# A searched order of steps and a rearranged prologue in a block-sparse attention and low-rank mixer kernel

## The chip, the cores and the metric

The kernel runs on one core of a Trainium2 chip. The core has TensorE (PE), VectorE (DVE), ScalarE (ACT), GpSimd (POOL) and SyncE (SP), and DMA queues that some of these issue to. The metric is the device time of one launch in microseconds. The median of three runs of the kernel before is 270.56 us (269.94 to 271.41).

## The reference

```python
scores = (1 / sqrt(64)) * q @ k.T            # 4 batches, 8 heads, 768 tokens, 64 channels
mask: blocks of 32 tokens; own block and both neighbours, first and last row and column of
      blocks, and three sampled blocks for each row of blocks
attn = softmax(where(mask, scores, -1e9)) @ v
x = attn as (batch, token, 512)
u = x + ((x.T @ U) @ V).T                    # U: 768 x 32, V: 32 x 768, over the tokens
out = u + relu(u @ w_ch1) @ w_ch2            # 512 -> 2048 -> 512
```

## The kernel before

**Tiling.** Two heads make a pair; there are 16 pairs, four for each batch. A head's 768 keys are six groups of 128 (the program's `g`), and scores are held with keys on the partitions and all 768 queries along the row. PSUM has eight banks of 512 fp32 columns; each step names the bank that it writes.

**The order of the work** is written out by hand, or by a search, in the string `PLAN`: one word for each step, from left to right, with the bank behind it where the step needs one. A capital without dots, or one of the words with dots, is TensorE's work; most lower-case letters are the VectorE or ScalarE operations that empty a bank. The program goes through the words and issues each step's instructions to its engine, so the list fixes the order on each engine; between engines only the dependencies count. A step that comes earlier in the string than one of another engine need not run earlier. The words that matter here:

- `S` (line 980) scores of one group, two banks; `B` (L999) scores of two groups, three banks; `e` the exponential of the oldest of them on ScalarE (L989, L1007). These serve pairs 0 to 3, batch 0. There the mask is added by the same matmul: below the 64 channels of `kres` stand rows with the mask's bias for each block (copied by `mask_row`, L287, out of a bank that `mask_half`, L279, fills), and below those of `qres` a one-hot row for each block.
- `A` six matmuls of a group's values (L414), `v` the division by the row sums (L544, L551).
- `R` the transposes of a later pair's queries or keys (L953), `t` their copies; `Z` those of the very first pair's second head (L352), `z` their copies (L359); `K`, `k` a part of the multiplicative mask for later batches.
- From pair 4 on: `Q` scores of one step of both heads, banks 0 to 5, on half the array's rows each (L1030), `e` the exponential (L1039), `p` the mask's multiplication on VectorE (L1045), `V` all six value products of a head.
- `M` and `D`, `E`, `F`, `X`, `Y` the mixer's products; `x`, `d` what adds and casts them in pairs 4 to 15 (L630, L634), `T` a transposing DMA of the result (SP, L623).
- `P`, `C`, `U` the up projection (L685), `a` and `b` its relu on ScalarE (L697) or VectorE (L699); with dots the last digit of `a` names the engine.
- `S`, `H`, `D` with dots: the down projection in seven products instead of eight, with sums of its inputs on VectorE (L721, L855) and the outputs' additions (L879). `q` sums of weights on VectorE, `g`, `c`, `o`, `r`, `s`, `h`, `e` with dots the last batch, where both projections are done in seven products; `t` with dots its input sums. `Z` with dots a store, `L` loads of a later pair.

**The prologue** (lines 243 to 346) stands before the list. `keep_warm` (L272) runs eight matmuls of constants. `first_cast` (L213) makes fp16 of the first head's queries and keys, `first_turn` (L227) transposes half of them with three matmuls on the identity, `first_row` (L293) copies 64 rows of the result out of the bank. Mask rows and key rows are read out of a bank partly by VectorE, partly by ScalarE. The second head of the pair is cast on GpSimd. `second_set` (L192) copies the one-hot and the mask rows to the second set of tiles by DMA from SP.

Of the kernel before, what the change touches and what calls it, by code (L numbers as in the profile page):

```python
# [12 lines left out]
FP32 = mybir.dt.float32  # L13
# [10 lines left out]
def kernel(  # L24
# [192 lines left out]
    def first_turn(n, c):  # L217

        if n == 1:
            pt = bank(5 + c, [P, HS], FP32)  # L220
        elif c == 0:
            pt = pw[:, 1, 0:HS]
        else:
            pt = psc2()[:, 0, 0:HS]
        first_out[n, c] = pt
        for j in range(3):
            nc.tensor.matmul(  # L227
                pt[0:D, j * P : (j + 1) * P],
                sts[0, ("qld", "kld")[n]][:, 3 * c + j, 0],
                id16,  # L230
                start=(j == 0), stop=(j == 2), skip_group_check=True,
            )

    with tc.manual_schedule(
# [27 lines left out]
        for vt in vts:  # L262
            nc.gpsimd.memset(vt[:, :, :, D : D + 1], 1.0)
# [12 lines left out]
        pks = [bank(2, [P, HS], FP32), bank(7, [P, HS], FP32)]  # L276
# [23 lines left out]
        keep_warm(8)  # L300
# [28 lines left out]
        mask_row(0, 1, nc.vector.tensor_copy)  # L329
        mask_row(1, 1, nc.vector.tensor_copy)  # L330
# [9 lines left out]
        load_mix_u()  # L340
        second_set()
# [117 lines left out]
    a.0.1.0.1 p a.0.1.14.1 Q v q.4.0 e V6 D.0.0.0 S.0.0.3 H.0.0.6.0 e v U.0.1.13.2 q.7.0 H.0.0.6.1
    U.0.1.12.6 a.0.1.13.1 D.0.0.2 y p Q a.0.1.12.1 q.5.1 H.0.0.7.0 e H.0.0.7.1 q.5.0 H.0.0.5.0.6 D.0.0.3  # L460
    H.0.0.5.1 e S.0.0.4.4 U.0.1.6.1 p H.0.0.4.0 a.0.1.6.1 H.0.0.4.1 D.0.0.4 Q D.0.0.5 p H.0.0.3.0 e L.7
    H.0.0.3.1 p H.0.0.2.0.7 H.0.0.2.1 e p U.0.1.8.2 U.0.1.15.0 D.0.0.1 D.0.0.6 a.0.1.8.1 V7 p a.0.1.15.1
    S.0.1.1.1 Q S.0.2.1.0 V6 e v S.0.1.2.4 H.0.1.1.0.7 y v H.0.1.1.1 y H.0.1.2.0.0 S.0.2.2.3 y H.0.1.2.1
    e D.0.1.0 M6 D.0.1.1 H.0.2.1.0.1 m H.0.2.1.1 S.0.2.3 F.1.0.2.4 D.0.2.0 F.1.1.3.6 F.1.2.5.0 x.6.0
    H.0.2.6.0 x.6.1 d.6.0 H.0.2.6.1 x.7.0 d.6.1 F.1.3.6.4 D.0.2.2 H.0.1.6.0 T.6 x.5.1 H.0.1.6.1 S.0.1.3
    H.0.2.7.0 H.0.2.7.1 x.4.0 H.0.2.5.0.6 x.5.0 H.0.2.2.0.0 D.0.2.3 d.5.0 H.0.2.2.1 x.4.1 d.5.1
    H.0.2.4.0 D.0.1.2 d.4.0 T.5 x.7.1 H.0.2.4.1 d.7.0 H.0.1.7.0 D.0.2.1 d.4.1 D.0.2.5 H.0.1.7.1 d.7.1
    S.0.2.4.2 T.4 Q D.0.1.3 H.0.2.5.1 e H.0.1.4.0 T.7 D.0.2.4 H.0.1.4.1 H.0.2.3.0 e D.0.1.5 H.0.2.3.1
    Z.0.0.1 p H.0.1.5.0.7 Z.0.2.1 H.0.1.5.1 D.0.2.6 Q Z.0.2.0 D.0.1.4 Z.0.0.0 S.0.1.4.0 U.1.0.0.6 e
    H.0.1.3.0 a.1.0.0.0 H.0.1.3.1 e U.1.0.11.6 D.0.1.6 p U.1.0.10.0 Z.0.1.0 Z.0.1.1 a.1.0.11.1 U.1.0.9.7  # L470
    p L.8 a.1.0.10.1 U.1.0.6.6 a.1.0.9.1 p Q a.1.0.6.1 p U.1.0.12.6 e V7 e U.1.0.2.2 v U.1.0.5.0 p
    a.1.0.12.1 U.1.0.1.7 a.1.0.5.1 a.1.0.2.1 U.1.0.3.6 a.1.0.1.0 p Q a.1.0.3.1 V6 p e U.1.0.4.7 v e
    U.1.1.5.2 a.1.0.4.0 U.1.0.15.6 p a.1.1.5.1 U.1.1.9.7 a.1.0.15.1 p Q a.1.1.9.1 U.1.1.3.7 e L.9
    U.1.0.7.6 a.1.1.3.0 e U.1.0.14.7 a.1.0.7.0 p U.1.1.4.0 U.1.1.10.6 a.1.0.14.1 a.1.1.4.0 U.1.1.1.7 p
    a.1.1.10.1 Q a.1.1.1.1 V7 e V6 v e U.1.1.7.7 v Q a.1.1.7.1 p U.1.0.8.7 e H.1.0.1.0.6 a.1.0.8.0
    H.1.0.1.1 p e U.1.1.13.7 p U.1.0.13.0 U.1.1.14.2 p a.1.0.13.1 a.1.1.13.1 U.1.1.8.3 S.1.0.1.3
    a.1.1.14.1 U.1.1.6.7 a.1.1.8.1 S.1.0.3 Q a.1.1.6.1 S.1.0.2.0 H.1.0.2.0.7 e D.1.0.0 L.10 H.1.0.2.1
    S.1.0.4.4 H.1.0.6.0 D.1.0.1 H.1.0.6.1 e U.1.1.15.1 U.1.1.11.0 a.1.1.15.0 U.1.1.0.7 p a.1.1.11.1 Q
    D.1.0.2 a.1.1.0.1 p y V7 e H.1.0.7.0 v e H.1.0.7.1 U.1.1.2.0 p U.1.1.12.7 D.1.0.3 a.1.1.2.1 p Q
    a.1.1.12.1 S.1.1.1.0 H.1.0.4.0 e H.1.0.4.1 S.1.1.2.1 V7 D.1.0.5 e S.1.1.3 H.1.1.1.0.6 p H.1.1.1.1 Q  # L480
    D.1.1.0 v H.1.1.6.0 e L.11 p H.1.1.6.1 H.1.0.5.0.7 D.1.1.2 H.1.0.5.1 e p H.1.1.7.0 H.1.1.7.1 D.1.0.4
    V0 y p y y H.1.1.5.0.3 S.1.1.4.3 y V4 y D.1.1.3 v H.1.1.5.1 v y H.1.1.4.0 H.1.1.4.1 S.1.2.1.1 y
    H.1.0.3.0 D.1.1.4 M4 S.1.2.2.0 H.1.0.3.1 m D.1.1.5 F.2.0.5.4 F.2.1.0.1 D.1.0.6 Z.1.1.1 H.1.2.1.0.6
    x.8.0 H.1.2.1.1 x.10.0 d.8.0 H.1.1.3.0 x.10.1 d.10.0 F.2.2.7.5 D.1.2.0 F.2.3.4.2 d.10.1 H.1.2.2.0.1
    x.8.1 T.10 H.1.2.2.1 x.11.0 H.1.1.3.1 x.9.0 d.11.0 H.1.2.6.0 x.11.1 d.8.1 H.1.2.6.1 d.9.0 D.1.1.6
    T.8 H.1.1.2.0.7 D.1.2.1 d.11.1 x.9.1 H.1.1.2.1 S.1.2.3 d.9.1 Q T.11 D.1.2.2 D.1.1.1 e H.1.2.7.0
    H.1.2.7.1 T.9 H.1.2.5.0.7 D.1.2.3 e H.1.2.5.1 S.1.2.4.2 H.1.2.4.0 Z.1.1.0 H.1.2.4.1 Z.1.0.1 Q
    D.1.2.5 D.1.2.4 U.2.0.4.6 p e H.1.2.3.0 a.2.0.4.0 H.1.2.3.1 e U.2.0.12.6 D.1.2.6 U.2.0.5.7 Z.1.2.0
    Z.1.0.0 a.2.0.12.1 Q Z.1.2.1 a.2.0.5.0 p U.2.0.2.7 e L.12 U.2.1.8.6 a.2.0.2.0 U.2.1.1.7 a.2.1.8.1 e
    U.2.0.11.2 a.2.1.1.0 U.2.0.15.6 p a.2.0.11.1 U.2.0.0.7 p Q a.2.0.0.1 p a.2.0.15.1 U.2.0.9.7 e V6  # L490
    a.2.0.9.0 p e U.2.0.8.0 v U.2.0.10.7 a.2.0.8.1 U.2.1.4.6 a.2.0.10.0 p Q a.2.1.4.1 V7 p e U.2.1.0.6 v
    e U.2.0.13.1 a.2.1.0.0 U.2.0.1.7 p a.2.0.13.1 U.2.1.2.6 a.2.0.1.1 p Q a.2.1.2.0 U.2.1.9.7 e L.13
    U.2.0.7.6 a.2.1.9.0 e U.2.0.6.7 a.2.0.7.0 p U.2.0.14.6 a.2.0.6.1 q.0.1 Q a.2.0.14.1 p V7 e q.0.0 V6
    v e q.1.1 U.2.0.3.7 v Q a.2.0.3.1 p H.2.0.1.0.7 e p U.2.1.5.6 H.2.0.1.1 S.2.0.1.4 e U.2.1.10.0
    a.2.1.5.0 U.2.1.14.1 S.2.0.2.1 a.2.1.10.0 U.2.1.3.6 a.2.1.14.1 D.2.0.0 Q S.2.0.3 a.2.1.3.1 p
    H.2.0.6.0 e H.2.0.2.0.6 p H.2.0.6.1 H.2.0.2.1 e D.2.0.2 U.2.1.13.0 D.2.0.1 S.2.0.4.3 H.2.0.7.0
    a.2.1.13.1 H.2.0.7.1 p y Q p V6 e D.2.0.3 H.2.0.4.0 v e H.2.0.4.1 V6 D.2.0.5 p Q v U.2.1.11.7 e
    H.2.0.5.0.6 a.2.1.11.0 H.2.0.5.1 q.1.0 e U.2.1.12.7 p U.2.1.15.0 p a.2.1.12.1 U.2.1.7.1 a.2.1.15.1
# [685 lines left out]
```

## Time and profile before

| | |
|---|---|
| median of three runs | 270.56 us |
| the profiled execution | 270.01 us |
| its span, first to last instruction | 268.2 us |
| mean granted TensorE clock | 0.999 |
| instructions | 7303 |
| first two-head score step | 42.76 us |
| first matmul of the last batch's up projection | 228.3 us |
| last matmul | 264.7 us |

A busy share is the time in which an engine had at least one instruction in work. TensorE's matmuls overlap: the profile gives each of them a duration of which a good part runs beside the next one. How close they follow is read from their starts. "Idle before", with an arrow, names what ended an engine's idle time. The lines are those of the program before.

### The profile page before, as it was taken

The page shows a single profiled execution, that of the slowest core. Times are in us where ns is not written, and L with a number is a line of the kernel's source. Part 1 is how long each engine was busy: PE and PEld are TensorE (multiplying, and loading weights), DVE is VectorE, ACT ScalarE, POOL GpSimd, SP SyncE. Part 2 cuts the span into 40 slices and gives each one's busy share as a digit, 9 for nine tenths or more (in the row PEclk, how much of TensorE's full clock was granted, in tenths as well). Part 3 has the DMA queues.
Part 4 walks back from the last instruction along what each step waited for, and adds up shares of the span by engine and source line. Part 5 has one row for each costly group of instructions (what it writes and reads, how often), then busy time and mean ns, then how long its engine had stood idle before and what let it go on. Part 6 is the DMA issues. An engine that isn't in the chain of part 4 may idle for free.

```text
span 268.2 us, 7303 instructions
## 1 busy us (share of the span) xinstructions
PE 262.4 (98%) x3006; PEld 182.4 (68%) x3006; DVE 232.5 (87%) x477; ACT 202.7 (76%) x265; POOL 72.7 (27%) x98
## 2 busy tenths in 40 slices
PE   8899999999999999999999999999999999999995
PEld 3677775555577778565666887555667788666884
DVE  5789988988999998868588997688998999999993
ACT  4999998897989667788898857788997944789200
POOL 4669006944462570070606160000000000000000
PEclk9999999999999999999999999999999999999999
DMA  6799997999999999897938997610200116400024
GB/s 192 245 324 263 207 235 123 113 135 144 189 146 133 117 103 111 284 98 89 90 39 67 106 109 139 223 34 13 51 0 2 42 42 117 159 2 0 2 98 137
DMA packets 88720, 31.66 MB, mean 118 GB/s; under 512 B 77104, under 2 KB 85840, under 8 KB 88688
## 3 DMA queue, kind: packets, MB, share of 16 engines
q0 software_dynamic: 49728, 10.10, 48.4%
q1 hardware_dynamic: 38492, 20.86, 33.6%
q8 instruction: 23, 0.38, 0.6%
q10 hardware_dynamic: 468, 0.26, 0.4%
q14 instruction: 9, 0.07, 0.1%
HBM read 27.67 MB, written 6.29 MB: 127 GB/s over the span
## 4 chain that ended last, share of the span: by engine, by line
PE 73%; DMA 12%; DVE 7%; ACT 2%; POOL 2%; issue 1%; SPq 0%; DVEq 0%; POOLq 0%; ACTq 0%
PE ps L760 32%; PE ps L685 17%; DMA w2t<-in_moe_w_ch_dram 9%; PE ps L414 9%; PE ps L1030 7%; DMA vld<-in_v_dram 2%; PE ps L999 2%; ACT est L1007 2%; PE ps L980 1%; DVE est L1045 1%; PE ps L272 1%; DMA qpl<-stqld 1%; PE ps L665 1%; DVE xf L551 1%; DVE res L969 1%
## 5 line engine op out<-in xcount | busy, mean ns | idle before, releaser
L1039 ACT ACTIVATE est<-ps 128x1536 f16<-128x1536 f32 x72 | 100.6, 1450 | 18.8 <-PE ps L1030 18.7
L685 PE MATMUL ps<-uT,w1t 128*128 128x384 f16 x384 | 70.2, 326 | 0.0
L1045 DVE TENSOR_TENSOR est<-est,mask 128x1440 f16<-128x1440 f16 x72 | 63.4, 903 | 0.6 <-ACT est L1039 0.2
L685 PEld LDWEIGHTS <-w1t 128*128 128x128 f16 x384 | 35.6, 97 | 26.6 <-issue 6.8
L414 PEld LDWEIGHTS <-est 128*128 128x128 f16 x1152 | 40.4, 97 | 7.0 <-issue 3.3
L414 PE MATMUL ps<-vt,est 128*128 128x65 f16 x1152 | 43.3, 193 | 0.2 <-DVE xf L551 0.2
L760 PEld LDWEIGHTS <-hid 128*128 128x128 f16 x358 | 34.0, 98 | 6.6 <-issue 1.6
L697 ACT ACTIVATE hid<-ps 128x384 f16<-128x384 f32 x63 | 29.7, 496 | 4.8 <-PE ps L685 4.3
L1030 PE MATMUL ps<-qpl,kpl 64*128 64x512 f16 (+1 forms) x288 | 31.7, 325 | 0.0
L139 POOL DMA_DIRECT2D stqld<-in_q_dram x20 | 16.3, 820 | 55.9 <-DMA qpl<-stqld 54.4
L760 PE MATMUL ps<-w2t,hid 128*128 128x256 f16 x238 | 31.1, 273 | 0.0
L879 DVE TENSOR_TENSOR xf<-xf,ps 128x256 f32<-128x256 f32 x63 | 25.4, 416 | 4.1 <-PE ps L760 3.7
L699 DVE TENSOR_SCALAR hid<-ps 128x384 f16<-128x384 f32 x33 | 18.3, 555 | 8.7 <-PE ps L685 8.0
L760 PEld LDWEIGHTS <-sums 128*128 128x128 f16 x216 | 20.1, 98 | 4.4 <-issue 1.0
L989 ACT ACTIVATE est<-ps 128x768 f16<-128x768 f32 x30 | 22.5, 812 | 0.1
L1030 PEld LDWEIGHTS <-kpl 64*128 64x128 f16 x288 | 12.3, 94 | 14.3 <-issue 9.1
L760 PE MATMUL ps<-res,sums 128*128 128x256 f16 x144 | 19.4, 273 | 0.0
L634 ACT CAST xh<-xf 128x384 f16<-128x384 f32 x24 | 11.0, 510 | 10.0 <-DVE xf L630 10.0
L551 DVE TENSOR_TENSOR xf<-ps,rcp 128x384 f32<-128x384 f32 x32 | 17.7, 554 | 0.8
L139 POOL DMA_DIRECT2D stkld<-in_k_dram x20 | 16.3, 819 | 1.9 <-issue 0.8
L139 POOL DMA_DIRECT2D vt<-in_v_dram x20 | 16.3, 820 | 0.0
L760 PE MATMUL ps<-res,hid 128*128 128x256 f16 x120 | 15.9, 273 | 0.0
(121 smaller groups left out, 339.3 us busy)
## 6 DMA issues: line engine op xcount, KB each, us to landing
out_dram<-xf SPq DMA_DIRECT2D x18, 256.0 KB, 2.4
vld<-in_v_dram SPq DMA_DIRECT2D x6, 384.0 KB, 6.3
w1t<-in_moe_w_ch_dram POOLq DMA_DIRECT2D x4, 512.0 KB, 8.3
w2t<-in_moe_w_ch_dram POOLq DMA_DIRECT2D x4, 512.0 KB, 12.1
qld<-in_q_dram SPq DMA_DIRECT2D x5, 384.0 KB, 3.7
kld<-in_k_dram SPq DMA_DIRECT2D x5, 384.0 KB
stqld<-in_q_dram POOLq DMA_DIRECT2D x20, 96.0 KB, 3.9
stkld<-in_k_dram POOLq DMA_DIRECT2D x20, 96.0 KB, 4.2
```

The costliest lines, as they stand in the source:

```text
L139: nc.gpsimd.dma_start(out=dst[:, h], in_=src[b, 2 * hp + h].rearrange("(p t) d -> p t d", t=T),)
L414: nc.tensor.matmul(pav[:, sc, :], est[:, n, sc * P : (sc + 1) * P], vts[b % 2][:, 2 * hp + h, g, 0 : D + 1], start=(g == 0 and sc == 0), s ...
L551: nc.vector.tensor_tensor(out=dst, in0=pav[:, :, 0:D], in1=rcp[:, :, None].broadcast_to([P, T, D]), op=ALU.mult,)
L685: nc.tensor.matmul(pt, w1t[:, cc, jj * P : (jj + 1) * P], bts[b].uT[:, cc, c * HS : (c + 1) * HS], start=(cc == 0), stop=(cc == NCC - 1), ...
L697: nc.scalar.activation(out=dst, in_=pt, func=AF.Relu)
L699: nc.vector.tensor_scalar_max(out=dst, in0=pt, scalar1=0.0)
L760: nc.tensor.matmul(acc[key], lhsT, rhs, start=(first and i == 0), stop=(i == len(pairs_) - 1), skip_group_check=True,)
L879: nc.vector.tensor_add(out=x, in0=x, in1=acc[a, b, tau])
L989: lambda: nc.scalar.activation(out=dst, in_=ps, func=AF.Exp, scale=0.125),
L1030: nc.tensor.matmul(units[h][:, u * S + lo : u * S + hi], kT[drows[h], g * P : (g + 1) * P], qT[drows[h], lo:hi], start=True, stop=True, sk ...
L1039: nc.scalar.activation(out=both[h], in_=units[h].rearrange("p (g n) -> p g n", g=2), func=AF.Exp, scale=0.125,)
L1045: lambda: nc.vector.tensor_mul(out=masked(both[h]), in0=masked(both[h]), in1=masked(mask[:, 2 * j : 2 * j + 2, :]),),
```

## The change

1. **Prologue, TensorE.** Eight warming matmuls of 512 columns become seven and one of 256. One of 128 columns is put behind the query turns, two behind the key turns. The turns take both heads' 128 columns as stationary operand (the second head's half is set to 1 first, by GpSimd) and write 128 rows, of which 64 are read as before.
2. **Prologue, readers.** Each bank is emptied by one engine: VectorE reads the first half of the mask rows and of the key rows, ScalarE the second half of the key rows. The second half of the mask and the mask rows of the second head go to a step of their own, `W`, the first word of the list, with three copies on VectorE; `second_set` and `load_mix_v` follow there.
3. **Fills and copies.** `Ut` is zeroed by GpSimd instead of VectorE, `Vt` behind the cast of `Ut`, the ones columns of the values behind the second head's casts. The one-hot copies of the second set are issued before `W`. The loads of pair 2 are issued with those of pairs 3 and 4 at the first step of pair 1, not at the first of pair 0; nothing else is issued from SP between.
4. **The list.** The same steps, besides `W`, in another order and in part on other banks, to the end of the program.

```diff
     def second_set():
         for h in range(2):
-            one_hot(1, h)
             nc.sync.dma_start(out=kres[1][mrows[h], h, :], in_=kres[0][mrows[h], h, :])
-        nc.sync.dma_start(out=kmask[mrows[0], :], in_=kres[0][mrows[0], 0, :])
+            if h == 0:
+                nc.sync.dma_start(out=kmask[mrows[0], :], in_=kres[0][mrows[0], 0, :])
...
+        nc.gpsimd.memset(Ut.bitcast(FP32), 0.0)
         nc.gpsimd.tensor_copy(out=Ut[:, :, 0:R], in_=uld)
+        nc.gpsimd.memset(Vt.bitcast(FP32), 0.0)
...
-                pt[0:D, j * P : (j + 1) * P],
-                sts[0, ("qld", "kld")[n]][:, 3 * c + j, 0],
+                pt[:, j * P : (j + 1) * P],
+                sts[0, ("qld", "kld")[n]][:, 3 * c + j].rearrange("p h d -> p (h d)"),
...
+        for nm in ("qld", "kld"):
+            nc.gpsimd.memset(sts[0, nm][:, :, 1], 1.0)
...
-        pks = [bank(2, [P, HS], FP32), bank(7, [P, HS], FP32)]
+        pks = [bank(2, [P, HS], FP32)]
...
-        keep_warm(8)
+        keep_warm(7)
+        keep_warm(1, 256)
...
         first_row(0, 1, nc.scalar.copy)
+        keep_warm(1, P)
         first_cast(0, 1, nc.vector.tensor_copy)
         mask_half(0)
         mask_row(0, 0, nc.vector.tensor_copy, 0, P)
-        mask_row(1, 0, nc.scalar.copy)
         first_turn(1, 0)
         first_row(1, 0, nc.vector.tensor_copy, 0, P)
-        first_row(1, 0, nc.scalar.copy, P, HS)
         mask_row(0, 0, nc.vector.tensor_copy, P, HS)
+        first_row(1, 0, nc.vector.tensor_copy, P, HS)
         first_turn(1, 1)
-        first_row(1, 1, nc.vector.tensor_copy)
-        mask_half(1)
-        mask_row(0, 1, nc.vector.tensor_copy)
-        mask_row(1, 1, nc.vector.tensor_copy)
+        first_row(1, 1, nc.scalar.copy)
+        keep_warm(2, P)
...
-        for tile_ in (Vt, kmask):
-            nc.gpsimd.memset(tile_.bitcast(FP32), 0.0)
-        nc.vector.memset(Ut, 0.0)
+        for vt in vts:
+            nc.gpsimd.memset(vt[:, :, :, D : D + 1], 1.0)
+        nc.gpsimd.memset(kmask.bitcast(FP32), 0.0)
         load_v(0)
         load_qk(1)
         load_v(1)
         load_mix_u()
+        for h in range(2):
+            one_hot(1, h)
+
+    def late_masks(n):
+        pks.append(bank(n, [P, HS], FP32))
+        mask_half(1)
+        for h, c in ((0, 1), (1, 0), (1, 1)):
+            mask_row(h, c, nc.vector.tensor_copy)
         second_set()
         load_mix_v()
...
     PLAN = """
-    S0 S3 e e S5 B0 e Z7 e S3 z Z6 e z A7 A B0 e R6 S3 t A R5 e A B0 t A K6 e A S3 k v A5 A e K6 k B0 A
...
-    q.7.1 U.0.1.4.6 e S.0.0.2.0 H.0.0.1.0.7 p H.0.0.1.1 a.0.1.4.1 U.0.1.0.0 p L.6 e U.0.1.14.1 q.4.1 V6
...
+    W7 S0 S5 e e S3 B0 Z6 z Z5 z e e S6 B3 S1 e e e R6 t A7 A A A A A v B0 e K3 k A5 R6 A A K7 S3 e t B0 e
...
+    U.0.1.7.7 a.0.1.7.0 U.0.1.2.6 a.0.1.2.1 U.0.1.9.7 a.0.1.9.1 Q e U.0.1.4.6 a.0.1.4.1 q.4.0 q.3.1 q.7.1 p
+    p S.0.0.2.0 e p p H.0.0.1.0.7 H.0.0.1.1 D.0.0.0 U.0.1.0.0 a.0.1.0.1 U.0.1.14.1 a.0.1.14.1 V6 v L.5 Q e e
...
-        for m in {0: (0,), 1: (1, 2), 3: (3,), 4: (4,)}.get(i, ()):
+        for m in {1: (0, 1, 2), 3: (3,), 4: (4,)}.get(i, ()):
...
+        "W": ((late_masks,) for _ in range(1)),
```

More of the change, by code (lines that the diff above doesn't have):

```diff
@@ L459 @@
[L459 to L488, printed above, removed]
@@ new lines @@
+    p p D.1.0.0 p U.1.1.8.7 a.1.1.8.1 U.1.0.13.1 a.1.0.13.1 S.1.0.1.3 S.1.0.2.0 S.1.0.4.4 U.1.1.14.2
+    a.1.1.14.1 U.1.1.13.5 a.1.1.13.1 U.1.1.6.7 a.1.1.6.1 Q e L.9 L.10 H.1.0.2.0.7 H.1.0.2.1 S.1.0.3
+    H.1.0.6.0 H.1.0.6.1 D.1.0.1 U.1.1.15.0 a.1.1.15.0 e p D.1.0.2 p U.1.1.11.1 a.1.1.11.1 U.1.1.0.7
+    a.1.1.0.1 Q e e V7 v y H.1.0.7.1 H.1.0.7.0 D.1.0.3 U.1.1.2.2 a.1.1.2.1 p p U.1.1.12.7 a.1.1.12.1
+    S.1.1.1.0 S.1.1.2.1 Q e e H.1.0.4.0 H.1.0.4.1 D.1.0.5 V7 S.1.1.3 p H.1.1.1.0.6 H.1.1.1.1 D.1.1.0 Q L.11
@@ new lines @@
+    U.2.0.10.6 a.2.0.10.0 p U.2.1.4.7 a.2.1.4.1 Q e e V7 v y U.2.1.0.6 a.2.1.0.0 U.2.1.2.1 a.2.1.2.0
+    U.2.0.1.7 a.2.0.1.1 U.2.0.13.6 a.2.0.13.1 Q e e p p U.2.1.9.7 a.2.1.9.0 U.2.0.7.6 a.2.0.7.0 U.2.0.6.7
+    a.2.0.6.1 U.2.0.14.6 a.2.0.14.1 L.12 L.13 Q e e p p V7 p V6 v y v U.2.0.3.7 a.2.0.3.1 S.2.0.1.4
+    S.2.0.2.1 Q e e U.2.1.5.6 a.2.1.5.0 S.2.0.3 H.2.0.1.0.7 H.2.0.1.1 D.2.0.0 U.2.1.14.0 a.2.1.14.1 y
+    U.2.1.10.1 a.2.1.10.0 p p p U.2.1.3.6 a.2.1.3.1 Q e e H.2.0.6.0 H.2.0.2.0.6 H.2.0.6.1 D.2.0.2 H.2.0.2.1
@@ new lines @@
+    S.2.2.2.1 H.2.2.5.0.3 H.2.1.7.0 F.3.0.2.6 x.14.0 d.14.0 F.3.1.4.5 x.12.1 d.12.1 x.14.1 d.14.1 T.14
+    x.12.0 d.12.0 T.12 H.2.1.5.0.1 H.2.2.6.1 H.2.2.6.0 D.2.2.2 H.2.2.5.1 F.3.2.5.6 x.13.0 d.13.0 x.15.0
+    d.15.0 F.3.3.2.4 x.15.1 d.15.1 x.13.1 d.13.1 T.13 H.2.1.7.1 D.2.1.3 H.2.1.5.1 H.2.2.7.1 H.2.2.7.0
+    D.2.2.3 H.2.2.2.0.4 H.2.2.2.1 D.2.1.4 S.2.1.4.2 D.2.2.4 H.2.1.4.1 H.2.2.4.0 D.2.2.1 S.2.2.4.3 q.6.1
+    H.2.1.4.0 D.2.1.5 T.15 H.2.2.4.1 t.1 D.2.2.5 Z.2.2.1 H.2.1.3.0 H.2.2.3.0 H.2.1.3.1 D.2.1.6 t.3 t.2 t.4
@@ L529 @@
+    e.2.6.1 e.2.6.0
     """
```

108 lines of the change are left out of this document (58 added, 50 removed).

## The prediction

> **What bounds the kernel now.** I read the page first, then the busy time by stages, then the order of the first 20 us.
>
> ```profile
> PE 262.4 (98%) x3006; PEld 182.4 (68%) x3006; DVE 232.5 (87%) x477; ACT 202.7 (76%) x265; POOL 72.7 (27%) x98
> ...
> PE 73%; DMA 12%; DVE 7%; ACT 2%; POOL 2%; issue 1%; SPq 0%; DVEq 0%; POOLq 0%; ACTq 0%
> ```
>
> TensorE is busy 98% of the span and is 73% of the chain that ended last. The same view by stages (stretch, length, then busy us and instructions of each engine) shows which engine stands beside it:
>
> ```profile
> 0.00:8.50 8.50, 7.22 (x33) 3.03 (x34) 5.59 (x17) 5.00 (x9) 3.89 (x13) 1.00 0.69 207
> 8.50:22.00 13.50, 13.04 (x189) 9.61 (x188) 10.79 (x24) 12.20 (x12) 9.19 (x11) 1.00 0.89 300
> 22.00:42.70 20.70, 20.34 (x307) 15.38 (x303) 18.68 (x42) 20.06 (x26) 7.90 (x11) 1.00 1.04 217
> ...
> 165.00:222.00 57.00, 56.93 (x694) 38.84 (x693) 49.12 (x89) 46.19 (x55) 0.00 (x0) 1.00 0.20 55
> 222.00:265.00 43.00, 43.00 (x346) 32.87 (x340) 40.21 (x108) 21.10 (x46) 0.00 (x0) 1.00 0.24 71
> ```
>
> Up to 42.7 us ScalarE's exponentials are as full as TensorE (20.06 of 20.70); later TensorE is alone at the limit, with VectorE close behind in the last stretch (40.21 of 43.00).
>
> A busy share hides short waits, because a matmul's record outlasts the start of the next: the L685 group has a mean of 326 ns, while in the chain "82.51 0.65 PE ps L685 x4" four follow each other in 0.65, 0.163 apart. So I summed, over all 3006 starts, what each start comes later than back to back. That is 21.8 us: 10.0 are 99 changes between matmuls on a part of the array's rows or columns (L1030, L665, L650, L227, L279) and full ones, 0.10 each; 11.9 are waits: 1.2 before 8.5 us, 2.2 to 22, 1.9 to 42.7, 2.9 to 75, 0.8 to 111, 1.1 to 165, 1.7 to 222 and 0.2 after that. Only the 11.9 can be gained by another order, since the two lists hold the same steps (one new word, W, aside), the same split of the relus between ScalarE and VectorE, and, followed through, the same number of those changes.
> The Trainium skill ("Trainium Kernel Development and Optimization", Performance Expectations) says the same of the matmul row: busy time is a poor measure because matmuls are pipelined. By the 98% alone at most 5.8 us could go, some 4 of them start and tail; by the starts it is 11.9, and I go by the starts.
>
> **The prologue.** Its rows:
>
> ```profile
> 0.78 3.57 PE L272 MATMUL ps<-const-bfloat16-1.0 128*128 128x512 bf16 x8 [0.78 <-PEq L1168]
> ...
> 3.47 0.36 DVE L213 CAST stqld<-qld 128x384 f16<-128x384 f32 x1 [0.52 <-DMA qld<-in_q_dram]
> ...
> 4.28 0.77 PE L227 MATMUL ps<-small,stqld 128*64 128x128 f16 x6
> ...
> 5.67 0.47 ACT L287 CAST res<-ps 24x384 f16<-24x384 f32 x1
> ...
> 6.17 0.42 DVE L287 CAST res<-ps 24x256 f16<-24x256 f32 x1 [0.22 <-ACT res L287]
> ...
> 6.54 2.23 ACT L989 ACTIVATE est<-ps 128x768 f16<-128x768 f32 x3
> ```
>
> The constant matmuls start 0.427 apart, so the halved eighth ends 0.21 sooner. The first cast is done at 3.47 + 0.36 = 3.83; the turns, at 4.28 now, then start at about 4.06: -0.21. They now fill all 128 columns, so one change of array shape goes (0.10), and the short matmul behind them costs 0.05 to 0.11: nothing in sum. The two short ones after the last turn lie in a wait for VectorE (below). GpSimd has to set the second heads' halves first: two fills of 0.3 to 0.75 each by its own rows (vt, res), done by 2.3 us, needed at 4.06. Its second-head casts must now wait for the turns (done near 4.9 and 5.6), but waited for their loads until 5.79 and 6.29: hidden by 0.7 at least.
>
> One reader for each bank: the row at 6.17 starts 0.03 after ScalarE's read of the same bank ends (5.67 + 0.47), with 0.22 idle. Now VectorE reads in a row: mask rows 0.29 from 5.19, key rows 0.28 to 5.73, mask rows 0.42 to 6.07, key rows (0.36 on ScalarE, I take 0.42) to 6.41. The first score then starts at 5.79 (now 6.01), its exponential at 6.32 (now 6.54); the next ones follow at ScalarE's own pace of 0.71. W's three row copies (0.55 each) run to 7.9 and delay nothing: the second head's rows (z) come at 9.01 today. The zeroing of Ut (0.38) leaves VectorE, that of Vt moves behind Ut's cast on GpSimd; they are first used at 18.45 (L572) and 22.57 (L603), against casts at 12.98 and 13.89. On SP the one-hot copies go ahead and the three copies of mask rows start after 7.9, as they did (7.82): nothing is late. Prologue: -0.2.
>
> **The first four pairs.** The turns of the second head now use banks 6 and 5, free at 7.85, so z comes at 8.41 and 8.96 (now 9.01 and 9.74) and its first double score at 9.55 instead of 10.36. But the list then puts a single score on banks 1 and 2, and the next double needs 0 to 2:
>
> ```profile
> 12.72 0.81 PE L999 MATMUL ps<-res 128*128 128x512 f16 x4 [0.18 <-ACT est L1007]
> ...
> 13.57 1.45 ACT L1007 ACTIVATE est<-ps 128x1536 f16<-128x1536 f32 x1 [0.20 <-PE ps L999]
> ...
> 15.07 0.81 PE L999 MATMUL ps<-res 128*128 128x512 f16 x4
> ```
>
> ScalarE: double from 10.50, single from 11.85, done at 12.66; the double score starts at 12.69 instead of 12.72. The lead of 0.8 is given back. From there to 20 us old and new list run the same ring: double score on banks 0 to 2, its exponential 0.85 later for 1.45, the next double score; 2.35 a round (12.72, 15.07, 17.42), whatever is placed between. From 22.1 to 37.7 exponentials follow without a gap in the old list, and the new one has the same singles there. I carry -0.2, the prologue's, to 42.7; the ends are -0.8 (the lead kept) and +0.5 (a second wait like that at 12.7).
>
> **From 42.7 to 222 us** the order of TensorE is the same over long stretches and else neighbours change places. Three places count. (a) Two two-head steps of pair 7 now follow one down step (0.44) after an up step on bank 2, whose relu takes 0.42 after 0.25: 0.23 each, 0 to +0.5; I take +0.2, as 0.10 of each is the change of array shape already counted. (b) Four weight sums (0.69 each, 2.8 of VectorE) move from the stretch around 195 to 212 us to that around 165 to 190; behind them the chain runs over VectorE from 210.6 to 219.4, and TensorE waits 1.7 in 165 to 222. I take -0.4, between 0 and -1.7. (c) VectorE stands until 74.63 for w2t, and TensorE at 79.73 for VectorE (0.24); the new list has two more sums (1.4) in front of that wait, but two masks behind it wait for ScalarE anyway: 0, between -0.3 and +0.5. Together -0.2, between -2.0 and +1.0.
>
> **Last stretch and tail.** With 0.2 us of waits there is nothing to gain. The last batch's four transposes start 1.33 apart and the last lands 2.8 after its start, at 228.17. The new list lets the first start after three additions (0.47 each) instead of two: 228.17 - 219.44 + 0.47 = 9.2 us after the batch's first mix parts, while the first product that needs all of them comes 18 down steps (0.436), three products (0.326) and the mix parts (0.7) after these, 9.5. Margin 0.3: cost 0 to +0.5, I take 0. At the end one more addition (0.33) stands close before the last two: +0.1.
>
> **Sum.** First 42.7 us -0.2, middle -0.2, last stretch and tail +0.1: -0.3. The profiled execution had 270.01 (span 268.2 and 1.8 around it), the median of the runs 270.56: 0.55 above. I forecast 270.56 - 0.3, some **270.2 us**.
>
> **Rivals.**
> 1. *The order frees the engine.* Waits of 8.5 to 222 us are 10.5 in all. If the many small swaps and moved sums take a quarter of them, against my three places, it is -2.6: 268.0. For it: VectorE and ScalarE lead the waits, and their work is moved to where they have slack. Against: the times that the same bank is used again are as tight in both lists.
> 2. *The last transposes come late* (slower). VectorE's input sums sit in front of the new list's last additions and wait for the last transpose. From a delay of 0.3 on every further one is lost, because nothing there is idle; one more place in the series, 1.33, costs 1.0: with the rest of the sum 271.3, and 271.9 where (a) and (c) cost their most.
> 3. *The clock opens a step later* (slower). Starts come twice as close from 4.8 us on (128 columns: 0.107 before, 0.055 after). If the shorter warming puts this off past the first scores, some 2.3 us of work up to 8.2 take twice as long; 1.2 of waits there absorb a part: +1.1 to +2.3, about 272. The Trainium skill ("TensorE: Matmul & The Clock Gate", Part 1, What's actually happening) has the clock follow activity in a free-running window of 3.4 us; by it the opening would also wander by itself, and no run here shows that yet.
> 4. *It does nothing*, since the lead at 9.5 us is lost at 12.7 and everything after is the old ring: 270.5, inside the forecast.
>
> **Chances.** Forecast with rival 4: 0.50; rival 1: 0.30; rival 2: 0.12; rival 3: 0.08. Within 0.5% (1.35 us, about what a measurement of this kernel can tell from no change) lies the first: faster 0.30, same 0.50, slower 0.20. The range, 267.8 to 272.0, takes in most of rivals 1 to 3; the likeliest case alone is 269.2 to 271.3.
>
> **What would show it.** Right: first exponential near 6.3, the double score near 9.5 and again one at 12.7; waits from 22 us on like today's; first two-head step (42.76) some 0.2 earlier; last matmul near 264.5. Wrong: a lead at 42.7 us over 0.8 (first pairs), waits between 42.7 and 222 that fall by over 1.5 (the middle), any gap in TensorE after 222 (transposes), starts still 0.107 apart after 5.1 us (clock).

## The result and the profile after

The changed kernel takes 274.32 us at the median of six runs (272.72 to 276.89), the kernel before 270.52 us on the same chip (269.94 to 272.2): a ratio of 1.0124, 95% interval 1.0083 to 1.0165. It is slower by 3.4 us (2.2 to 4.5), where 0.3 us less was forecast and the range ended at 272.0. The profiled execution took 273.40 us, with a span of 271.6 us (before: 268.2). Ratios compare fast runs alone: of each kernel they leave out the runs over 1.5% above its fastest, and the profiled run of three_mended is such a one.

The page's first part and the chain's shares hardly differ from before:

```profile
PE 262.8 (97%) x3009; PEld 181.4 (67%) x3009; DVE 232.4 (86%) x477; ACT 202.3 (74%) x264; POOL 73.8 (27%) x101
...
PE 73%; DMA 13%; DVE 4%; ACT 4%; issue 2%; POOL 2%; SPq 1%; DVEq 0%; ACTq 0%; POOLq 0%
```

TensorE works 0.4 us longer in a span that is 3.4 longer: it waits. Summed over all starts as in the prediction, the waits rose from 11.9 to 14.9 us, and the changes of array shape fell from 99 to 96 (10.0 to 9.65 us). The list of waits of the new kernel's TensorE (us in total, times, longest) says for what:

```profile
PE ps L691 <- DMA uT<-xh: 1.2, 1, 1.2
PE ps L423 <- DVE est L1051: 1.1, 1, 1.1
PE ps L274 <- PEq L1175: 0.8, 1, 0.8
PE ps L986 <- ACT res L295: 0.4, 1, 0.4
PE ps L986 <- DVE res L295: 0.4, 1, 0.4
```

These are the first five of eight lines; the other three are 0.2 to 0.4 each. The third is the start and was there before. The other four belong to three places, and the same step's start in both traces dates them: the first two-head step went from 42.76 to 43.41 us (+0.65), a later one from 113.07 to 114.83 (+1.76), the last product of uT and w1t ahead of the last batch from 210.21 to 213.09 (+2.88), the last matmul from 264.73 to 267.82 (+3.1).

**Place 1, the prologue (+0.65).** Timeline of the new kernel (start, busy us, engine and line):

```profile
4.81 0.66 PE L281 MATMUL ps<-res,bias 24*128 24x384 f16 x2
5.35 0.76 DVE L289 CAST res<-ps 24x128 f16<-24x128 f32 x2 [0.77 <-PE ps L281]
5.41 0.51 PE L229 MATMUL ps<-small,stkld 128*128 128x128 f16 x6
...
6.48 0.50 PE L986 MATMUL ps<-res 128*128 128x384 f16 x2 [0.45 <-ACT res L295]
7.01 2.41 ACT L995 ACTIVATE est<-ps 128x768 f16<-128x768 f32 x3 [0.59 <-PE ps L986]
```

Both mask matmuls stand ahead of the turn of the keys: the second is W's, the list's first word. So the list's first step does not stand behind the prologue's text on its engines; why the built program has it so, no run shows. In the group at 5.35 a copy of W's mask rows (0.545 from 5.56) stands ahead of the key rows, which it delays to 6.14. The first exponential starts at 7.01, against 6.54 before and 6.32 in the forecast.

**Place 2, the landing of w2t (+1.1).** A transfer is issued when an engine hands it to a queue, and it has landed when the last of its sixteen parts is done. VectorE's weight sum and TensorE's values, first before, then after:

```profile
77.48 1.26 PE L414 MATMUL ps<-vt,est 128*128 128x65 f16 x36
...
74.63 0.69 DVE L721 TENSOR_TENSOR w2t<-w2t 128x1024 f16<-128x1024 f16 x1 [0.24 <-DMA w2t<-in_moe_w_ch_dram]
```

```profile
74.14 0.68 DVE L727 TENSOR_TENSOR res<-w2t 128x1024 f16<-128x1024 f16 x1
76.32 0.69 DVE L727 TENSOR_TENSOR w2t<-w2t 128x1024 f16<-128x1024 f16 x1 [1.49 <-DMA w2t<-in_moe_w_ch_dram]
...
80.12 0.54 PE L423 MATMUL ps<-vt,est 128*128 128x65 f16 x12 [1.09 <-DVE est L1051]
```

The two sums put ahead of it cost nothing; VectorE stands idle for 1.49 behind them. The last of w2t's four loads landed at 76.22 instead of 74.54, and two masks stand behind the sum that needs it.

**Place 3, the last transpose of batch 2 (+1.2).** SyncE's queue and the first product of the batch's next half, first before, then after:

```profile
161.03 5.54 SPq L623 DMA_TRANSPOSE uT<-xh  x4
...
168.36 0.82 PE L685 MATMUL ps<-uT,w1t 128*128 128x384 f16 x4
```

```profile
162.25 2.55 SPq L629 DMA_TRANSPOSE uT<-xh  x2
164.85 1.04 SPq L713 DMA_DIRECT2D out_dram<-xf  x2
165.99 2.60 SPq L629 DMA_TRANSPOSE uT<-xh  x2
```

```profile
169.93 0.66 PE L691 MATMUL ps<-uT,w1t 128*128 128x384 f16 x3
171.80 0.32 PE L691 MATMUL ps<-uT,w1t 128*128 128x384 f16 x1 [1.21 <-DMA uT<-xh]
```

Two stores of the new list stand between the transposes, which before were issued in one row from 161.03 to 166.57. The last, issued at 167.36, landed 4.40 later; before it took 2.75.

### The profile page after: what moved, and what is told of

Read it like the earlier page. It is cut to its first block, busy times and chain, and to the rows that moved or that the text cites. A ratio compares the mean times of both kernels' runs of the same rounds, so it can differ in the third digit from the quotient of the medians.

```text
span 271.6 us, 7316 instructions
## 1 busy us (share of the span) xinstructions
PE 262.8 (97%) x3009; PEld 181.4 (67%) x3009; DVE 232.4 (86%) x477; ACT 202.3 (74%) x264; POOL 73.8 (27%) x101
## 4 chain that ended last, share of the span: by engine, by line
PE 73%; DMA 13%; DVE 4%; ACT 4%; issue 2%; POOL 2%; SPq 1%; DVEq 0%; ACTq 0%; POOLq 0%
PE ps L766 32%; PE ps L691 17%; PE ps L423 10%; DMA w2t<-in_moe_w_ch_dram 8%; PE ps L1036 7%; PE ps L986 2%; ACT est L1013 2%; DMA vld<-in_v_dram 2%; DMA uT<-xh 2%; DMA qpl<-stqld 2%; ACT est L995 1%; PE ps L274 1%; PE ps L1005 1%; PE ps L671 1%; DVE est L1051 1%
## 5 line engine op out<-in xcount | busy, mean ns | idle before, releaser
L1051 DVE TENSOR_TENSOR est<-est,mask 128x1440 f16<-128x1440 f16 x72 | 62.5, 901 | 0.9 <-ACT est L1045 0.9
L423 PEld LDWEIGHTS <-est 128*128 128x128 f16 x1152 | 39.1, 97 | 7.8 <-issue 3.9
L423 PE MATMUL ps<-vt,est 128*128 128x65 f16 x1152 | 41.8, 193 | 1.1 <-DVE est L1051 1.1
```

Of the source, the lines that this page charges most:

```text
L423: nc.tensor.matmul(pav[:, sc, :], est[:, n, sc * P : (sc + 1) * P], vts[b % 2][:, 2 * hp + h, g, 0 : D + 1], start=(g == 0 and sc == 0), s ...
L1051: lambda: nc.vector.tensor_mul(out=masked(both[h]), in0=masked(both[h]), in1=masked(mask[:, 2 * j : 2 * j + 2, :]),),
```

## The experiments

Times are medians of the interleaved runs; each ratio is against the kernel before, with its 95% interval. "Theory" was at first: three separate places, 0.65 + 1.1 + 1.2.

**Halves of the list.** The lists come to the same state after 290 new and 289 old words, at about 66 us.

```
 new_front_old_rest: new prologue, PLAN = new words 1 to 290 + old words from 290 on
 old_front_new_rest: old prologue, PLAN = old words 1 to 289 + new words from 291 on
```

> The new prologue and the new list up to 66 us (its first 290 steps), and the old list from there on. Theory (three places: the mask rows of W ahead of the first score +0.65, two weight sums ahead of the sum that waits for w2t with two masks behind it +1.1 at 73 to 80 us, two stores between the last transposes of batch 2 +1.2 at 170 to 176 us): only the first is left, so the first exponential starts near 7.0, the first two-head score near 43.4, and the time is 0.65 above the kernel before, some 271.2 us. Rival (the new list is tighter from end to end, and what is late anywhere stays late): the delay grows behind the cut as well, 272 or more. Rival (the delay of the first pairs is absorbed by the slack of the old list behind it): 270.5.

> The old prologue and the old list up to 66 us, and the new list from there on. Theory: the second and third place are left, the first two-head score at 42.76 as before, 1.1 more by 80.6 us and 1.2 more by 179 us, with 0.3 at the end: 2.3 to 2.8 above the kernel before, 272.9 to 273.3 us. Rival (the places are a consequence of the late start, which shifts the transfers against the engines): no more than 1 above before, 271.5 or less.

Measured: 271.38 us, 1.0036 (1.0011 to 1.0061), and 271.23 us, 1.0027 (1.0008 to 1.0045). Each half costs 0.3%, both together 1.24%: they do not add, and my three places are not three independent prices. The new front with the old rest shows the wait of place 3 without the new stores between the transposes:

```profile
169.48 0.34 PE L690 MATMUL ps<-uT,w1t 128*128 128x384 f16 x1
170.81 0.65 PE L690 MATMUL ps<-uT,w1t 128*128 128x384 f16 x3 [0.99 <-DMA uT<-xh]
```

The old front with the new rest has the stores between them and no such wait in its profiled run (269.98). So the stores alone are not it; something else meets the last transpose. (That run is the fastest of its twelve; what the slower ones waited for was not traced.)

**W where the text has it.**

```
         first_row(1, 1, nc.scalar.copy)
         keep_warm(2, P)
+        pks.append(bank(7, [P, HS], FP32))
+        mask_half(1)
+        for h, c in ((0, 1), (1, 0), (1, 1)):
+            mask_row(h, c, nc.vector.tensor_copy)
...
-    W7 S0 S5 e e S3 B0 ...
+    S0 S5 e e S3 B0 ...
```

> The new kernel, with the mask matmul and the three row copies of W put where the text of the prologue puts them, behind the copies of the first four turns, instead of as the list's first step. Theory: PE and DVE no longer hold them ahead of the second turn of keys and its copies; the first score at 5.8 and the first exponential at 6.3 to 6.6 (7.0 in the new kernel), the first two-head score at 42.6 to 42.9 (43.4): 0.5 to 0.8 under the new kernel, 273.5 to 273.8 us. Rival (the copies into the four banks are late for another reason, the banks or the clock): first exponential still at 6.9 or later, time as the new kernel's, 274.3.

Measured: 274.25 us, 1.0129 (1.0098 to 1.0159). The first exponential came at 6.43 and the first two-head step at 42.756, as the theory had it, and nothing of it was left at the end: w2t landed at 76.89 and TensorE waited 2.3 in place 2, 1.7 of it at once. Here a start that the transfers did not follow was lost at the next wait for one.

**The sums behind the masks.**

```
-    ... a.0.1.4.1 q.4.0 q.3.1 q.7.1 p p S.0.0.2.0 e p p H.0.0.1.0.7 ...
+    ... a.0.1.4.1 p p S.0.0.2.0 e p p q.4.0 q.3.1 q.7.1 H.0.0.1.0.7 ...
```

> The new kernel, with the three weight sums q.4.0, q.3.1 and q.7.1 moved behind the two pairs of masks and the score between them that stood behind them on the engine. Theory: the masks no longer stand behind the wait for w2t (1.5 us on VectorE), the wait of the matmuls at 80.1 for the masked exponentials (1.09) goes: 0.9 to 1.2 under the new kernel, 273.2 us, with the two-head turn of 80.59 at 79.5. Rival (the sums hold the engine for as long wherever they stand, 0.69 each, and the masks or the normalisations behind them are late then): under 0.4 back, 274 us.

Measured: 273.99 us, 1.0155 (1.0115 to 1.0195): nothing back. The wait at 80 us went (the two-head step at 79.48, 35.91 after the first; before, 35.92), and TensorE waited 1.6 for VectorE's additions behind the three sums instead. The rival was right.

**Other numbers of instructions on TensorE.** The trace has packets of an instruction queue: 23 of 16 KB, on average some 255 of TensorE's records apart (156 to 399 in the kernel before). One lies at 169.69 in the new kernel, 2.3 behind the issue of the late transpose; in the kernel before it lies at 169.52, 4.2 behind. To move it, the warming matmuls were cut finer:

```
 (new_front_old_rest)            (before)
-        keep_warm(7)           -        keep_warm(8)
+        keep_warm(28, P)       +        keep_warm(31, 112)
```

> The kernel of new front and old rest, whose last transpose of batch 2 landed 4.3 after its issue (2.75 in the kernel before) with a 16 KB packet of the instruction queue 2.1 after that issue, and whose TensorE waited 1.0 for it. Here 28 warming matmuls of 128 columns stand in place of 7 of 512: the same 3.0 us, and 42 more instructions on TensorE, so that the fetches, which come every 256 of them, come 1.7 us earlier. Theory (the fetch and the last transpose collide): the fetch lies 0.4 after the issue, the transpose lands 2.8 after it, the wait at 170 goes, and the time is 0.7 to 1.0 under that kernel's 271.4: 270.4 to 270.7. Rival (the transposes come too late behind the late front, whatever the fetch does): landing 4.3 after the issue again, wait 1.0, 271.4.

> The kernel before with 31 warming matmuls of 112 columns in place of 8 of 512 (3.3 us against 3.4), which is 46 more instructions on TensorE and nothing else. Its fetch at 169.52 lies 4.2 behind the issue of the last transpose of batch 2 and should move to 2.15 behind it. Theory (collision of fetch and transpose): that transpose lands 4.3 after its issue instead of 2.75, TensorE waits 0.8 to 1.0 for it at 169 to 170, and the kernel before gets as much slower, 271.0 to 271.3. Rival: nothing changes, 270.2.

Measured: 271.65 us, 1.0041 (1.0023 to 1.0059), no better than its parent, and 271.15 us, 1.0042 (1.0016 to 1.0068), slower as forecast. The second is right by luck in the main: in its profiled run 0.84 of the loss is there by the first two-head step (43.59), and the wait for the transposes is 0.3, not the 0.8 to 1.0 forecast. And neither packet moved as I had counted: the packet came 1.1 behind the issue of the last transpose in both, not 0.4 and 2.15. There it lay 2.5 behind the issue of the third, and now the third landed late (4.5 after its issue instead of 2.8) and the fourth by 0.9; the wait was 0.4 and 0.3. In both runs the lateness moved with the packet, from the fourth transpose to the third; by how much a count of instructions moves the packet is not shown.

**w2t's loads first.**

```
     def loads(i):
         if HP + 1 < i + 1 < NPAIR:
             front(i + 1)
+        if i in (HP, HP + 1):
+            load_w2(range((i - HP) * NJJ // 2, (i - HP + 1) * NJJ // 2, 4))
         if i + 2 < NPAIR:
             load_qk(i + 2)
...
-        if i in (HP, HP + 1):
-            load_w2(range((i - HP) * NJJ // 2, (i - HP + 1) * NJJ // 2, 4))
```

> The new kernel with the loads of w2t issued ahead of the loads of q, k and v of the same step on GpSimd's queue, 5 us earlier. Theory (what the masks at 74 to 80 us wait for is the landing of w2t, late since the DMA engines are busy throughout): w2t lands before VectorE asks for it at 74.8, the 1.5 of idle VectorE and the 1.1 of TensorE at 80.1 go, first two-head score to the turn of 80.6 in 35.9 (37.2 in the new kernel, 35.9 before), time 1.0 to 1.3 under the new kernel: 273.1. Rival (the sums themselves are too many ahead of the masks): VectorE does not idle but TensorE still waits 0.7 or more at 80. Rival (the loads of q and k are pushed back instead): a new wait for the transposes of the pairs behind, nothing gained.

Measured: 275.18 us, 1.0149 (1.0112 to 1.0186). Place 2 went (35.92 from the first two-head step to that of 79 us), so the landing was its cause; but in this run the first two-head step came at 44.63, against 43.41 in the new kernel, and the time did not fall. The first mask matmul waited 0.3 for a constant's load, and TensorE came late to its full rate: matmuls of 384 columns still started 0.320 apart at 8.8, where the new kernel has 0.162 from 7.6 on, and the granted clock is recorded as full only from 9.64, against 5.19.

**The prologue without the new list.**

```
 new prologue with W in text order, PLAN = the old list (new_prologue_old_list)
 the same, PLAN = "W7" + the old list                   (new_prologue_old_list_w)
```

> The new prologue, with the mask matmul and row copies of W where the text puts them, and the whole old list. Theory (the prologue is worth what was forecast, and the losses come from the new list and from W's place): first exponential 6.3 to 6.6, first two-head score 42.5 to 42.8, 270.0 to 270.3. Rival (the chain of transfers, not the engines, decides what follows, and the two memsets added on GpSimd and the later first loads delay it): the first two-head score as before but waits at 75 to 80 or at 170, 270.8 to 271.5.

> The new prologue with the old list, as in the run of 270.31, but with W as the list's first step, as the change has it. Theory: both mask matmuls stand ahead of the second turn of keys, the first exponential at 7.0, the first two-head score at 43.0 to 43.2, and the time 0.6 to 0.8 above that kernel's: 270.9 to 271.1. Rival (the wait it makes is given back behind it): 270.3.

Measured: 270.31 us, 0.9997 (0.9974 to 1.002), and 270.54 us, 1.0021 (1.0006 to 1.0037). The times of the prologue in order are near those forecast:

```profile
4.62 0.33 PE L281 MATMUL ps<-res,bias 24*128 24x384 f16 x1
4.88 0.51 PE L229 MATMUL ps<-small,stkld 128*128 128x128 f16 x6
...
5.71 0.50 PE L984 MATMUL ps<-res 128*128 128x384 f16 x2
6.24 2.34 ACT L993 ACTIVATE est<-ps 128x768 f16<-128x768 f32 x3 [0.34 <-PE ps L984]
```

The first exponential is at 6.24 and the first two-head step at 42.42 (before: 6.54 and 42.76). With W at the list's head they are at 6.92 and 43.10. The price of W's place at the end, 0.2% by the two ratios, is within their intervals.

But the 0.30 at the first exponential cannot be put down to the prologue. The clock is recorded as full from 4.35 in this run and from 4.83 in that of the kernel before, and matmuls of 128 columns start 0.107 apart ahead of that and 0.055 behind it. Like compared with like, and runs aside that waited for a constant's load: where the full clock came at 4.75 to 4.83, the first exponential is at 6.43 and 6.44 with the new prologue in order (w_in_text_order, three_mended) and at 6.54 with the old one; where it came at 3.83 to 4.12, at 6.26 to 6.28 (two_mended, placed_stores_behind, placed_front_old_rest) and at 6.14 with the old one (old_front_stores_behind). Between these the prologue's own gain is 0.1 either way, and the medians, 270.31 for both kernels, show none.

**Two mends, three mends, and the stores alone.** three_mended has all three edits, two_mended leaves the stores.

```
-    ... d.10.1 d.10.0 T.10 Z.1.0.0 Z.1.1.1 H.1.2.1.0.6 ...
+    ... d.10.1 d.10.0 T.10 H.1.2.1.0.6 ...
-    ... D.1.2.5 Q e e T.9 p T.11 U.2.0.4.6 ...
+    ... D.1.2.5 Q e e T.9 p T.11 Z.1.0.0 Z.1.1.1 U.2.0.4.6 ...
```

> The new kernel with W's mask matmul and row copies in text order, and with w2t's loads ahead of those of q, k and v. Each alone gave nothing at the median (274.25 and 275.2 against 274.3): the first lost its 0.65 again waiting for w2t, the second fell on a late prologue. Theory (two losses, one behind the other, so that both must go): first two-head score 42.4 to 42.8, that score to the turn at 79 us in 35.9, and the time 1.8 under the new kernel, 272.3 to 272.8, with the wait for the last transpose of batch 2 (1.2) still there. Rival (the new list is late wherever the transfers are, and new waits come): 273.5 or more.

> As the one with two mends, and with the two stores Z.1.0.0 and Z.1.1.1 behind the last two transposes of batch 2, which are then issued 1.1 earlier, while the fetch of TensorE's instructions stays where it is. Theory: the fetch lies 3.4 behind the last transpose's issue instead of 2.3, it lands 2.8 after its issue, and the wait at 170 goes: 1.2 less again, 271.1 to 271.5. Rival (the late transposes are not what the batch waits for): 272.3 or more, as with two mends.

> The new kernel with the two stores alone behind the transposes. Theory (the last transpose, issued 1.1 earlier, misses the fetch): landing 2.8 after its issue, wait at 170 gone, 1.0 to 1.2 under the new kernel: 273.1. Rival (the chain of work from the late w2t decides, and the wait comes out as another behind it): 274 or more.

Measured: 274.42 us, 1.0133 (1.009 to 1.0176) with two mends, 274.32 us, 1.0095 (1.0054 to 1.0137) with three, and 272.26 us, 1.0059 (1.0028 to 1.0089), with the stores moved alone. The waits of two_mended's TensorE show what w2t's early loads did:

```profile
PE ps L1033 <- DMA kpl<-stkld: 2.1, 1, 2.1
PE ps L688 <- DMA uT<-xh: 1.1, 1, 1.1
```

The transpose of the keys that it waits for was issued at 56.63, against 52.27 in the new kernel, and landed at 67.50 instead of 65.65, as the rival had it: the transfers change places. This wait has a second price. From 68.7 to 72.1 the granted clock is 0.50, and 36 products of the values take 2.18 instead of 1.26; by the rows of that stretch I estimate that it cost some 1.5 more. three_mended waited 3.0 for the same keys and has the same 0.50 from 69.7 to 73.1; no other profiled run has such a stretch between its start and its end, and none of them waited more than 1.7 at once.

The stores alone bring back half of the loss. That their place counts is clearest in the two kernels with W in text order, where the intervals lie apart: 1.0129 (1.0098 to 1.0159) above, and 1.0045 (1.0023 to 1.0068) with the stores moved too, below. The last transpose lands 2.77 after its issue and the four matmuls run through:

```profile
163.93 5.53 SPq L627 DMA_TRANSPOSE uT<-xh  x4
```

```profile
171.62 0.82 PE L689 MATMUL ps<-uT,w1t 128*128 128x384 f16 x4
```

Its profiled run, 1.5 above its median, shows another wait of the same kind. A store issued at 115.63 had its first part done at 119.34 and its last at 121.69, with a 16 KB instruction packet at 119.18. As I read it, VectorE may not overwrite the tile before that, and TensorE waits for VectorE:

```profile
121.87 0.56 DVE L555 TENSOR_TENSOR xf<-ps,rcp 128x384 f32<-128x384 f32 x1 [1.89 <-issue]
122.48 1.25 PE L423 MATMUL ps<-vt,est 128*128 128x65 f16 x36 [1.63 <-DVE xf L555]
```

The profile puts VectorE's idle time down to "issue"; it ends 0.18 after the store's last part.

**The same early loads on the old list.** Edit: new_prologue_old_list with the edit of w2_ahead.

> A try for the best of both: the new prologue with W in text order, the old list, and w2t's loads ahead of those of q, k and v. Theory: the 0.24 of VectorE's wait for w2t goes, TensorE gains 0 to 0.2: 270.0 to 270.3. Rival (q and k of the pairs behind land later by the 5 us that w2t gains, and are waited for): 270.6 or more.

Measured: 272.89 us, 1.0106 (1.0068 to 1.0144), the rival: new waits of 1.1 for the keys' transposes and 1.0 in place 3.

**What adds up.** placed_stores_behind: the stores moved and W in text order. old_front_stores_behind: old_front_new_rest with the stores moved. placed_front_old_rest: new_front_old_rest with W in text order.

> The new kernel with the two stores behind the transposes and W in text order; w2t's loads stay where they were. Theory (the stores' place is worth 2.1 at the median, and W's 0.65 is lost again in the wait for w2t): 272.0 to 272.4, the first two-head score at 42.8, TensorE's wait at 80 us grown to 1.7 or more. Rival (W's place is worth its 0.65 once the transposes are in time): 271.6 or less.

> The kernel of old front and new rest (271.23, half of its runs at 270.1 and half at 271.1 to 272.3), with the two stores behind the transposes. Theory (its runs above 270.2 are those in which the fetch meets the last transpose, issued 2.5 ahead of it): with the transpose 1.1 earlier the runs draw together at 270.0 to 270.4, and the last transpose lands 2.8 after its issue. Rival (what makes the new rest slower lies elsewhere): 271.2.

> The kernel of new front and old rest (271.38) with W in text order. Theory (its loss is W's place, not the order of the new list up to 66 us): first two-head score at 42.7, 270.3 to 270.8. Rival (the later first casts and loads of the new front keep the transfers late, and with them the transposes of batch 2 in the way of the fetch): 271.2 or more.

Measured: 271.73 us, 1.0045 (1.0023 to 1.0068); 270.17 us, 1.0017 (0.9996 to 1.0038); 270.86 us, 1.0026 (1.0008 to 1.0044). The first undoes some two thirds of the loss with two edits of the list. TensorE's wait at 80 us was 0.4 there, not the 1.7 expected, since w2t landed at 75.09. The second is level with the kernel before: its median fell by 1.06 against old_front_new_rest, with 7 of 12 runs at 269.6 to 270.2, though by the ratios (1.0027 and 1.0017) the two cannot be told apart. The third is neither forecast; its profiled run names a further transfer:

```profile
11.93 0.51 PE L957 MATMUL ps<-small,stqld 128*128 128x128 f16 x6 [1.16 <-POOL stqld L131]
```

The load behind that cast, issued at 3.85 in every kernel, landed at 9.45 to 10.99 in the profiled runs.

**The best of the parts.** Edit: old_front_stores_behind with the new prologue and W in text order.

> The parts that cost nothing put together: the new prologue with W in text order (270.31 with the old list), the old list up to 66 us, the new one from there on with the two stores behind the transposes (270.17 with the old prologue). Theory (the prologue's 0.3, seen in one trace, lasts to the end): 269.7 to 270.0. Rival (the loads of the second pair, which land between 9.7 and 11.0, take the lead back in most runs): 270.1 to 270.4, no better than the kernel before.

Measured: 271.69 us, 1.0057 (1.0032 to 1.0082), worse than either part and than both theories. Its profiled run waited 0.6 for a constant's load ahead of the first mask matmul, with the first two-head step at 43.23; why most of its runs are late stays open. No version was faster than the kernel before by more than its interval.

**The packet and the last transpose, in all profiled runs** (us; "behind" is from the issue of batch 2's last transpose to the packet):

```
kernels                                                packet behind  packet's time  lands after issue  TensorE waits
before, three_mended, old_front_stores_behind,
  best_of_parts                                        3.0 to 4.3     0.88 to 1.18   2.75 to 2.79       0
old_front_new_rest                                     2.52           1.02           2.78               0
new_prologue_old_list, placed_front_old_rest,
  placed_stores_behind, stores_behind                  2.28 to 2.58   1.46 to 1.94   2.75 to 2.77       0
after, new_front_old_rest, w_in_text_order,
  sums_behind_masks, w2_ahead, two_mended,
  prologue_old_list_w2, new_prologue_old_list_w        2.01 to 2.46   0.88 to 1.13   4.30 to 4.48       1.0 to 1.3
more_short_warm, before_short_warm                     1.07 to 1.10   0.93           3.64 to 3.67       0.3 to 0.4
```

Where the two meet, one of them is late: the transpose by 1.6, or the packet by 0.5 to 1.0. From 2.28 to 2.46 behind, both cases occur, and what decides between them is not shown. In six of the eight runs with 4.3 to 4.5 only the last of the transpose's sixteen parts is late (in the new kernel fifteen had landed by 170.18, and the last came at 171.76, 1.2 behind the packet's end); in sums_behind_masks and w_in_text_order all sixteen are. Neither the order of the stores sorts these runs (among those with 2.8 and among those with 4.3 some have the stores between the transposes and some have not) nor the front alone (new ones stand in both, an old one in none of the runs with 4.3).

## Why the prediction was wrong, point by point

- **What bounds the kernel** held: the loss is in TensorE's waits (11.9 to 14.9), and 97% busy hid it.
- **Rival 3, the clock,** did not make the profiled run of the change slow: its turn of the keys at 5.41 already ran at 0.055 a matmul. But the start of the full clock does wander, which the prediction had as not yet seen: it is recorded at 3.39 to 6.36 in the other profiled runs and at 9.64 in w2_ahead, where the first two-head step came 1.2 later than in the new kernel. The latest four all have the new prologue, but only four runs have the old one, so whether the shorter warming matters stays open.
- **Prologue, -0.2.** Not confirmed for the prologue itself (0.1 either way between runs with a like start of the full clock; the -0.30 of one trace is luck), and wrong for the change: the step "W's three row copies (0.55 each) run to 7.9 and delay nothing" failed. It took the list's first word to run behind the prologue's text; the trace has W's matmul and one copy ahead of the keys, +0.47 there and +0.65 at 42.7.
- **First four pairs, -0.2 carried.** The lead is lost as described, but a load of the second pair, 9.45 to 10.99, can take it too, which I did not price.
- **Middle (c), "0, between -0.3 and +0.5".** The masks waited for w2t, not for ScalarE: 1.1. The sums in front cost nothing, as I had it; the failing step is the landing time, which I kept at 74.63. It came 1.68 later. From 45 to 78 us the DMA engines are busy throughout: in the run of the kernel before, w2t's loads of 512 KB take 9 to 12 us from issue to landing and the transposes of q and k 10 to 13 (2.75 for a transpose at 165 us), so a late start is not made up. The halves have it near the old time (new front with old rest 74.50, old front with new rest 74.17), the kernels with both, w2t's loads in their old place, at 75.09 to 76.89; but with W in order the new front and old rest had 75.50, behind a wait of 1.2 at 11.93. What of the 1.68 comes from a late start and what from the order is not settled.
- **Middle (a), (b).** Nothing in the traces is due to them: the two-head steps of pair 7 show no new wait, and of the 0.4 forecast for the moved sums 0.06 came (the two-head steps are 2.94 late at 174 and 2.88 at 213); the stretch from 165 to 222 lost 1.2 to place 3.
- **Rival 2** named the mechanism, late last transposes with nothing idle behind, but put it into the last batch, where the margin of 0.3 held: landing at 231.50, 9.3 after the batch's first mix parts, and no wait for them. It struck in batch 2, where the two stores in between, which I had not followed along SyncE's queue, put the last transpose 5.1 behind the first instead of 4.3. That step stood in the sum at nothing, without a reason, and is the largest: with the stores moved the loss is 0.59% instead of 1.24%. The stores are not the whole mechanism, since the packet decides with them: in the profiled run with the stores moved it still came 2.58 behind the issue, and was itself late (1.94).
- **Tail, +0.1**: 0.34 from the last batch's mix to the last matmul and 0.3 behind it.
- **The sum.** I added places as if each kept its price. The experiments say otherwise: 0.3% and 0.3% for the halves, 1.24% for the whole; W's mend worth nothing alone and, behind the stores' mend, 0.14% within the intervals. With both mends 0.45% stays, and I have no experiment that divides it between w2t, the first loads, the clock and the tail.

## What to carry over

In a kernel whose main engine has no idle time, follow every DMA that a new order moves along its own queue, and look up when it lands, not only when its engine is free: an earlier engine just waits longer for it. Price a transfer with a margin that covers its late runs (here 1.6 us for a transpose that takes 2.75). Compare the first microseconds of two kernels only between runs in which the full clock came at the same time. And read where the first instructions of a list really stand in the trace before counting on the order of the text.

## What the runs showed of the hardware

Instruction packets and data transfers hold each other up, as the table and the two runs with finer warming have it. In the table a 16 KB packet takes 0.9 to 1.2 us, and 1.5 to 1.9 where it is the late one; a transfer that meets it has its last part done 1.6 us late (the transposes at 170), and a store met in the same way had 2.35 us between its first part and its last (121.69). Where the packet falls depends on the program: 42 to 46 more matmul and weight-load instructions at the start moved it by 1.0 and 3.1 us against the transposes, not by the same amount.

A long wait of TensorE can cost more than itself. Behind waits of 2.1 and 3.0 us the granted clock was 0.50 for 3.4 us (two_mended, three_mended); behind waits of up to 1.7 it was not. Single runs of other kernels also record a mean clock of 0.985 to 0.994 (two of the twelve with the stores alone moved, three of six of w2_ahead), where one stretch of 3.4 us at 0.50 in some 270 gives 0.994, by my estimate; that these runs had such a wait is not shown.

Runs of one kernel differ, and more so in the new order. The kernel before keeps within 269.6 to 270.4 in most runs; old_front_new_rest has runs at 270.0 to 270.1 and, but for one, others at 270.8 to 272.3, and the changed kernel, but for one, spreads over 272.7 to 275.4. That transfers close to being waited for make this spread is my reading; no run separates it from the clock. One profile shows one of these cases, so its waits name the mechanism, and only the medians give the price.
